# A fifth buffer for the probabilities of an attention stage, and one subtraction moved from VectorE to GpSimd

## The chip, the cores and the metric

The kernel runs on one core of a Trainium2 chip. The metric is the device time of one execution in microseconds, from a program that does everything in one launch. Engines are named as the profile names them: PE is TensorE's matmul, PEld its weight load, DVE is VectorE, ACT is ScalarE, POOL is GpSimd, SP is SyncE, whose queue issues most DMAs.

## The reference

Three parts in a row. Attention comes first, over 2 batches of 8 heads with 768 positions of 64 values: queries and keys are hashed to 6 bits by the signs of a projection, and a query sees only the keys of its own bucket.

```python
mask = q_bucket[:, :, :, None] == k_bucket[:, :, None, :]
scores = scale * np.matmul(q, k.transpose(0, 1, 3, 2))
scores = np.where(mask, scores, -1000000000.0)
scores = scores - np.max(scores, axis=-1, keepdims=True)
attn = np.exp(scores)
attn = attn / (np.sum(attn, axis=-1, keepdims=True) + 1e-09)
return np.matmul(attn, v).astype(np.float32)
```

Its rows go through a mixture of 8 experts (each token to one expert by a gate, two matmuls with a ReLU between), and the result through a dense layer of 2048 with `h * clip(h + 3, 0, 6) / 6`. All is fp32.

## The kernel before

fp32 accuracy is made from faster operand types: a number is split into a high half, rounded to the type of the operand, and a low half, the rest, and products of halves are summed. In attention a head's queries and keys come in as one tile `r` of 128 x 768 (64 rows of queries over 64 of keys). `halves` makes `hi` on ScalarE as `r` scaled by `SC`, and a tile for `lo`; the low half is `r * SC - hi`. It is made in `prep0` for heads 0 to 2 and in `prep` for the others. Four tiles of a set (X, Y, K1, K2; four sets, head modulo 4) get the halves: ScalarE writes the high ones of heads 0 to 2, `send_low` sends the low ones by two DMAs from SP's queue (L378, L379). `hi` (heads other than 1) and `lo` each have one buffer, so the next head's waits for the last one's readers.

For heads 0 and 1 GpSimd subtracts (L392) after ScalarE has made a scaled fp32 copy `x`. For head 2 VectorE does it in one instruction, scale and subtraction together (`low_half`, L374), as it does for all heads after it.

A head's 768 keys are 6 blocks, so there are 96 steps k over the 16 heads. In each step

- `mx` (eight steps ahead, more in the first steps) gives the row maxima: two matmuls (L456), each reduced by VectorE (L459), over three PSUM buffers. After a head's sixth block `turn` transposes the maxima and sends them from SP's queue as row 76 of that head's X (L470), where `scores` reads it;
- `scores` does four matmuls (L480, L481) into two PSUM buffers, and ScalarE takes the exponential of each half into `pf`, a block of fp32 probabilities of 128 x 768 (L482);
- `high` rounds `pf` to f16 on ScalarE (L487; every few blocks on VectorE, L489), and `low` subtracts on GpSimd (L493; at the end of the stage mostly on VectorE), which frees `pf`;
- `pv` multiplies the halves of two blocks with the values in every second step (L508 to L510).

The tag `pf` of pool `pt` has four buffers, taken in turn. Its first users, in program order, are `fill`, the scaled copy of head 0, `hi` of head 1, the scaled copy of head 1, and then the blocks 0, 1, 2 and so on.

The order of each engine's queue is written out by hand: straight code ahead of the loop (L744 to L812), then a loop over k in which `due(k)` runs what `at(...)` and `spread(...)` have put at a step or a fraction of one (table `Q`). Each engine works its queue in order. The scale of the values (`vscale`, a chain of small VectorE instructions and three small matmuls) ends with `isw` on VectorE (L649), and GpSimd copies that tile in place (L804) before it goes on to the loop. The low half of head 2 and its two sends stand at step 5.0, the load of the values of heads 4 to 7 (`load_v`, L599) at step 4.0.

After attention come the routing of the tokens, the experts (L1066 to L1302) and the dense layer (L1305 to L1455).

Of the kernel before, what the change touches and what calls it, by code (L numbers as in the profile page):

```python
# [9 lines left out]
F32 = mybir.dt.float32  # L10
F32R = mybir.dt.float32r
# [3 lines left out]
ALU = mybir.AluOpType  # L15
# [4 lines left out]
P = 128  # L20
B, H, S, D = 2, 8, 768, 64
NH = B * H
BITS = 6
NC = S // P
# [4 lines left out]
E = 8  # L29
# [13 lines left out]
SC = 2.0**-17  # L43
# [20 lines left out]
def moe_attention_kernel(ctx, tc, qk, v, vt, pj, wg, w1, w2, win, wout, out, cap):  # L64
    nc = tc.nc
    pe, act, dve, pool, sp = nc.tensor, nc.scalar, nc.vector, nc.gpsimd, nc.sync
# [3 lines left out]
    def opened(stack, name, bufs, side="left", **kw):  # L70
        return stack.enter_context(tc.tile_pool(name=name, bufs=bufs, side=side, reuse_waits="tile", **kw))

    def f32(t):
        return t.bitcast(F32)

    def run(gen):
        for _ in gen:
            pass
# [104 lines left out]
    def rtile(shape, name, dt=F32):  # L183
        return r1.tile([P] + shape, dt, tag=name, name=name)

    def bc(a, n):
        return a.unsqueeze(len(a.shape)).to_broadcast(list(a.shape) + [n])

    def mid(a, n):
        return a.unsqueeze(1).to_broadcast([a.shape[0], n] + list(a.shape[1:]))  # L190

    oh = rtile([B, NC, E], "oh", F16)
    rs = rtile([B, E], "rs", F16)
# [122 lines left out]
    with ExitStack() as actx:  # L316
# [3 lines left out]
        pt = opened(actx, "pt", 2)  # L320
# [33 lines left out]
        pf_t, phi_t, plo_t, pv_t, xp_t = {}, {}, {}, {}, {}  # L354
        vr_t, vt_t, vh_t, am_t, sc_t, sw_t = {}, {}, {}, {}, {}, {}

        def misc(name):
            return ps_x.tile([P, 512], F32, tag="x", name=name)

        def load_r(h):  # L360
            rt[h] = pr.tile([P, S], F32, tag="r", name=f"r{h}")
            sp.dma_start(out=rt[h], in_=qk[h])

        def halves(h):
            r = rt[h]
            if h == 1:
                hi = pt.tile([P, S], F32, tag="pf", name=f"hi{h}", bufs=4).bitcast(F32R)
            else:
                hi = ph.tile([P, S], F32R, tag="hi", name=f"hi{h}", bufs=1)
            act.activation(hi, r, AF.Copy, scale=SC)  # L370
            return r, hi, ph.tile([P, S], F32R, tag="lo", name=f"lo{h}")

        def low_half(lo, r, hi):
            dve.scalar_tensor_tensor(out=lo, in0=r, scalar=SC, in1=f32(hi), op0=ALU.mult, op1=ALU.subtract)  # L374

        def send_low(h, lo):
            st = sets[h % 4]
            sp.dma_start(out=f32(st["K1"])[D:P], in_=f32(lo)[D:P])  # L378
            sp.dma_start(out=f32(st["Y"])[0:D], in_=f32(lo)[0:D])  # L379

        def prep0(h):

            r, hi, lo = halves(h)
            if h < 2:
                x = pt.tile([P, S], F32, tag="pf", name=f"rs{h}", bufs=4)
                act.activation(x, r, AF.Copy, scale=SC)
            for n, d, o in (("X", 0, 0), ("K2", 0, D), ("K1", 0, D), ("Y", D, 0)):
                if h or n in ("K1", "Y"):
                    act.activation(sets[h][n][d : d + D], r[o : o + D], AF.Copy, scale=SC)
            yield  # L390
            if h < 2:
                pool.tensor_tensor(out=lo, in0=x, in1=f32(hi), op=ALU.subtract)  # L392
            else:
                low_half(lo, r, hi)
            yield
            send_low(h, lo)

# [74 lines left out]
        def scores(k):  # L472
            h, j = divmod(k, NC)
            st = sets[h % 4]
            pf = pf_t[k] = pt.tile([P, S], F32, tag="pf", name=f"pf{k}", bufs=4)
            kc = slice(j * P, (j + 1) * P)
            for n in range(2):
                ps = ps_t.tile([P, 512], F32, tag="t", name=f"pst{k}{n}")
                qc = slice(n * HS, (n + 1) * HS)
                pe.matmul(ps[:, :HS], st["K1"][:, kc], st["Y"][:, qc], start=True, stop=False)  # L480
                pe.matmul(ps[:, :HS], st["K2"][0:77, kc], st["X"][0:77, qc], start=False, stop=True)  # L481
                act.activation(pf[:, qc], ps[:, :HS], AF.Exp, scale=0.125 / SC / SC)  # L482
# [64 lines left out]
        def rows_of(r):  # L547
            b, k = divmod(r, KD)
            return xd[1 + b * S : 1 + (b + 1) * S, k * P : (k + 1) * P].rearrange("(p c) d -> p c d", c=NC)
# [113 lines left out]
        def unmatched(r):  # L663

            b, k = divmod(r, KD)
            rows = rows_of(r)
            n = 2 * NC * D
            vt = pr.tile([P, S], F32, tag="r", name=f"uv{r}").rearrange("p (h c d) -> p h c d", h=2, c=NC)
            sp.dma_start(out=vt.rearrange("p h c d -> p (h c d)"), in_=v[:, r * n : (r + 1) * n])
            last = r == NH // 2 - 1  # L670
            if not last:
                x = pr.tile([P, S], F32, tag="r", name=f"ux{r}").rearrange("p (c d) -> p c d", c=NC)
                sp.dma_start(out=x, in_=rows)
            m = pt.tile([P, S], F32, tag="pf", name=f"um{r}", bufs=4)
            ps = misc(f"psu{r}")
            for c in range(NC):
                pe.matmul(ps[:, 0:P], ones, vt[:, :, c], start=c == 0, stop=c == NC - 1)
            act.activation(m[:, 0:P], ps[:, 0:P], AF.Copy, scale=1.0 / S)
            ps = misc(f"psc{r}")
            pe.transpose(ps[:, 0:P], m[:, 0:P], ident)  # L680
            act.activation(m[:, P : 2 * P], ps[:, 0:P], AF.Copy, scale=SW)
            ps = misc(f"psl{r}")
            pe.matmul(
                ps[:, 0 : 2 * E], m[:, P : 2 * P], wg_sb[:, k, 0:2].rearrange("p h e -> p (h e)"), start=True, stop=True
            )
            z = nm[:, 2 * r : 2 * r + 2].rearrange("p h c -> p c h")
            y = pt.tile([P, S], F32, tag="pf", name=f"uy{r}", bufs=4).rearrange("p (c h d) -> p c h d", c=NC, h=2)
            dve.tensor_tensor(
                out=y, in0=bc(z, D), in1=mid(m[:, 0:P].rearrange("p (h d) -> p h d", h=2), NC), op=ALU.mult
            )  # L690
            if last:

                x = xp_t[r][:, :, E : E + D]
                dve.tensor_tensor(out=x, in0=x, in1=y[:, :, 0], op=ALU.add)
                sp.dma_start(out=rows[:, :, 0:D], in_=x)
                x = pv_t[2 * r + 1][:, 0 : NC * VA].rearrange("p (c d) -> p c d", d=VA)
                t, n = y[:, :, 1], nm[:, 2 * r + 1]
                dve.tensor_scalar(
                    out=t, in0=t, scalar1=sc_t[r // 2][:, 0:1], scalar2=float(S), op0=ALU.mult, op1=ALU.mult
                )  # L700
                dve.tensor_tensor(out=x[:, :, 0:D], in0=x[:, :, 0:D], in1=t, op=ALU.add)
                dve.scalar_tensor_tensor(
                    out=x[:, :, DE], in0=n, scalar=float(S), in1=x[:, :, DE], op0=ALU.mult, op1=ALU.add
                )
            else:
                dve.tensor_tensor(out=x, in0=x, in1=y.rearrange("p c h d -> p c (h d)"), op=ALU.add)
                sp.dma_start(out=rows, in_=x)
            y = pt.tile([P, S], F32, tag="pf", name=f"uz{r}", bufs=4)[:, 0 : NC * 2 * E]
            y = y.rearrange("p (c h e) -> p c h e", c=NC, h=2)
            dve.tensor_tensor(  # L710
                out=y, in0=bc(z, E), in1=mid(ps[:, 0 : 2 * E].rearrange("p (h e) -> p h e", h=2), NC), op=ALU.mult
            )
            for hh in range(2):
                dve.tensor_tensor(out=lg[:, b], in0=lg[:, b], in1=y[:, :, hh], op=ALU.add)
# [26 lines left out]
                pool.tensor_copy(c, c)  # L741


        fill = pt.tile([P, S], F32, tag="pf", name="fill", bufs=4)  # L744
        neg, zrow = fill[0:1], fill[32:33]
        pool.memset(neg, -1.0)
        pool.memset(zrow, 0.0)
# [14 lines left out]
        pre = [prep0(h) for h in range(3)]  # L762
        for n in range(2):
            for i, t in enumerate(("X", "K2")):
                c = slice(n * HS, (n + 1) * HS)
# [39 lines left out]
        heat(ps_v, "v", 2)  # L805
        mx(NC)
        run(pre[1])
        load_r(4)
        put_bits(2)
        first = vsplit(0), vgate(0)  # L810
# [22 lines left out]
        def at(k, f, *args):  # L833
            later.setdefault(k, []).append((f, args))
# [11 lines left out]
        def stages(gen, ks):  # L846
            for k in ks:
                at(k, next, gen, None)

        stages(first[0], (2, 2))  # L850
        stages(first[1], (2, 2.5, 3, 3.5, 4.5))
        at(5.0, run, pre[2])
        for i in range(3):
            at(Q["lr"][i], load_r, 5 + i)
        for g in range(1, G):
# [18 lines left out]
        for h in range(NH):  # L874
            k = NC * h + NC - 1 + LAG
# [63 lines left out]
        h = NH - 1  # L939
# [251 lines left out]
    def heat(n):  # L1191
# [23 lines left out]
        out=gates, in0=ps2[:, :, NW:], scalar=1.0 / LS, in1=gates, op0=ALU.mult, op1=ALU.add  # L1215
# [37 lines left out]
    for e in range(E):  # L1253
# [30 lines left out]
        for s in range(KF):  # L1284
            d, half = divmod(s, 2)
# [173 lines left out]
    with ExitStack() as octx:  # L1459
        op = opened(octx, "op", 1)  # L1460
# [128 lines left out]
```

## Time and profile before

| | us |
|---|---|
| median of 3 runs | 653.27 |
| lowest and highest | 651.11, 654.57 |
| the profiled execution | 653.98 |
| its span, first to last instruction | 652.3 |
| TensorE busy in the span | 623.4 |
| VectorE busy | 478.8 |
| ScalarE busy | 435.9 |
| GpSimd busy | 234.0 |

The durations that are used come from the profiled execution; what it took beyond its span lies around the first and last instruction. A matmul's duration holds its way through the array, so matmuls overlap, and a busy TensorE is read together with its waits. Attention takes the first third of the span.

### The profile page before, as it was taken

The numbers are of one execution on the slowest core, as the hardware profiler recorded it, in microseconds if no ns is written. First come the engines' busy times: TensorE is split into PE (matmuls) and PEld (weight loads), VectorE is DVE, ScalarE is ACT, GpSimd is POOL, SyncE is SP. The second block draws the span as 40 slices with busy tenths as digits, with TensorE's granted clock in tenths as the row PEclk, the third lists the DMA queues.
The fourth block names the chain that finished last, engine by engine and source line by source line (L and its number), as shares of the span: only waits on it lengthen the run. The fifth ranks groups of instructions, "written<-read, shape, count | busy, mean of one in ns | idle before, by whom it ended". The sixth has DMA issues, their size and how long they took to land.

```text
span 652.3 us, 14467 instructions
## 1 busy us (share of the span) xinstructions
PE 623.4 (96%) x5530; PEld 452.5 (69%) x5530; DVE 478.8 (73%) x1056; ACT 435.9 (67%) x882; POOL 234.0 (36%) x222
## 2 busy tenths in 40 slices
PE   8999999999998799999999999999999999999892
PEld 3678788788887589999999985555555555555441
DVE  6889998898999888888988887888887332222410
ACT  8878888788888657677777745554445685555820
POOL 6666978978994142210866100000000020000021
PEclk9999999999999999999999999999999999999997
DMA  6658568656474188877677553444440020000011
GB/s 196 204 137 230 166 159 230 167 132 179 100 203 145 36 286 276 250 248 238 207 241 252 164 170 117 135 129 140 151 131 31 1 81 17 1 1 0 2 50 53
DMA packets 35732, 92.19 MB, mean 141 GB/s; under 512 B 6778, under 2 KB 12250, under 8 KB 35650
## 3 DMA queue, kind: packets, MB, share of 16 engines
q1 hardware_dynamic: 32562, 83.75, 43.2%
q0 software_dynamic: 2400, 7.36, 3.4%
q8 instruction: 46, 0.75, 0.5%
q14 instruction: 36, 0.29, 0.1%
q10 hardware_dynamic: 688, 0.03, 0.1%
HBM read 67.14 MB, written 6.29 MB: 113 GB/s over the span
## 4 chain that ended last, share of the span: by engine, by line
PE 56%; DMA 4%; ACT 3%; issue 1%; DVE 1%; POOL 0%; POOLq 0%; DVEq 0%; ACTq 0%
PE psg L1363 17%; PE pso L1390 15%; PE psy L1141 11%; PE psh L1114 11%; DMA out_dram<-os,inv 3%; ACT junk L1317 2%; PE psa L1091 1%; ACT gh L1373 1%; DVE rl L1366 1%; DMA xg<-xd,ids 1%; DMA xd<-xp 1%; ACT rl L1365 0%; POOL xg L1072 0%; ACT xp L944 0%; POOL out_dram L1405 0%
## 5 line engine op out<-in xcount | busy, mean ns | idle before, releaser
L493 POOL TENSOR_TENSOR plo<-pf,phi 128x768 f16<-128x768 f32 x86 | 145.3, 1713 | 19.7 <-DVE phi L489 10.0
L1405 POOL DMA_INDIRECT out_dram<-os,inv x12 | 12.1, 1012 | 272.6 <-DVE os L1397 244.5
L482 ACT ACTIVATE pf<-pst 128x384 f32<-128x384 f32 x192 | 83.1, 486 | 30.0 <-PE pst L481 25.3
L459 DVE TENSOR_REDUCE mx<-psm 128x1 f32<-128x384 f32 x192 | 96.0, 546 | 6.8 <-PE psm L456 6.6
L164 DVE SCALAR_TENSOR_TENSOR wl<-raw,wh 128x1024 f16<-128x1024 f32 (+1 forms) x68 | 83.4, 1230 | 5.8 <-ACT wh L158 5.1
L1363 PE MATMUL psg<-yTh,ch 128*128 128x512 f16 (+1 forms) x256 | 83.4, 326 | 3.2 <-DVE rl L1366 3.2
L1363 PE MATMUL psg<-yTl,ch 128*128 128x512 f16 (+1 forms) x256 | 83.4, 326 | 0.0
L1363 PE MATMUL psg<-yTh,cl 128*128 128x512 f16 (+1 forms) x256 | 83.4, 326 | 0.0
L1366 DVE SCALAR_TENSOR_TENSOR rl<-rl,psg 128x512 f32<-128x512 f32 x64 | 35.0, 551 | 64.4 <-ACT rl L1365 64.0
L480 PE MATMUL pst<-Y,K 128*128 128x384 f32 x192 | 74.9, 390 | 2.5 <-ACT pf L482 2.5
L1363 PEld LDWEIGHTS <-ch 128*128 128x128 f16 x512 | 50.1, 98 | 35.9
L487 ACT ACTIVATE phi<-pf 128x768 f16<-128x768 f32 x85 | 71.7, 844 | 1.9
L1390 PE MATMUL pso<-ch,gh 128*128 128x512 f16 x192 | 72.8, 379 | 0.0
L1390 PE MATMUL pso<-ch,gl 128*128 128x512 f16 x192 | 72.8, 379 | 0.0
L1390 PE MATMUL pso<-cl,gh 128*128 128x512 f16 x192 | 72.8, 379 | 0.0
L158 ACT ACTIVATE wh<-raw 128x1024 f16<-128x1024 f32 (+1 forms) x68 | 67.4, 998 | 0.5 <-issue 0.5
L1390 PEld LDWEIGHTS <-gh 128*128 128x128 f16 x384 | 37.6, 98 | 42.3
L1141 PE MATMUL psy<-hh,wl 128*128 128x224 f16 x256 | 66.3, 259 | 0.0
L1141 PE MATMUL psy<-hl,wh 128*128 128x224 f16 x256 | 66.3, 259 | 0.0
L1141 PE MATMUL psy<-hh,wh 128*128 128x224 f16 x256 | 66.3, 259 | 0.0
L481 PE MATMUL pst<-X,K 77*128 77x384 f32 x192 | 65.4, 341 | 0.6 <-DMA X<-rm 0.6
L508 PE MATMUL psv<-vh,phi 128*128 128x73 f16 x576 | 64.0, 197 | 0.0
(251 smaller groups left out, 1477.2 us busy)
## 6 DMA issues: line engine op xcount, KB each, us to landing
raw<-in_w_dram SPq DMA_DIRECT2D x64, 512.0 KB
rc<-in_win_dram SPq DMA_DIRECT2D x16, 512.0 KB
rc<-in_wout_dram SPq DMA_DIRECT2D x16, 512.0 KB
r<-in_qk_dram SPq DMA_DIRECT2D x16, 384.0 KB
K<-hi SPq DMA_DIRECT2D x26, 192.0 KB
vr<-in_v_dram SPq DMA_DIRECT2D x4, 768.0 KB
vt<-in_vt_dram SPq DMA_DIRECT2D x8, 384.0 KB
K<-lo SPq DMA_DIRECT2D x16, 192.0 KB
```

Of the source, the lines that this page charges most:

```text
L158: act.activation(wh[e, i][:, c : c + n], r, AF.Copy, scale=(S1, S2)[i // 2])
L164: dve.scalar_tensor_tensor(out=wl[e, i][:, c : c + n], in0=r, scalar=(S1, S2)[i // 2], in1=wh[e, i][:, c : c + n], op0=ALU.mult, op1=ALU.s ...
L459: dve.tensor_reduce(out=mm[:, c, n : n + 1], in_=ps[:, :HS], axis=AX.X, op=ALU.max)
L480: pe.matmul(ps[:, :HS], st["K1"][:, kc], st["Y"][:, qc], start=True, stop=False)
L481: pe.matmul(ps[:, :HS], st["K2"][0:77, kc], st["X"][0:77, qc], start=False, stop=True)
L482: act.activation(pf[:, qc], ps[:, :HS], AF.Exp, scale=0.125 / SC / SC)
L487: act.activation(phi_t[k], pf_t[k], AF.Copy)
L493: eng.tensor_tensor(out=plo_t[k], in0=pf_t.pop(k), in1=phi_t[k], op=ALU.subtract)
L1114: pe.matmul(ps, l[:, c], r[:, k], start=n == 0, stop=n == 3 * KD - 1)
L1141: pe.matmul(ps, l, r, start=n == 0, stop=n == 3 * KF - 1)
L1363: pe.matmul(ps, l, x, start=n == 0, stop=n == 3 * KD - 1)
L1390: pe.matmul(po[blk][s], l, r, start=first and n == 0, stop=last and n == 2)
```

## The change

The tag `pf` gets a fifth buffer. The low half of head 2 is made as those of heads 0 and 1 are, in two instructions, but both on GpSimd: it scales `r` into a `pf` buffer (the fifth in turn) behind the low half of head 1, and subtracts behind the copy of `isw`. The sends of that low half go from step 5.0 to step 4.0, where they stand ahead of the load of the values of heads 4 to 7.

```diff
         def halves(h):
             r = rt[h]
             if h == 1:
-                hi = pt.tile([P, S], F32, tag="pf", name=f"hi{h}", bufs=4).bitcast(F32R)
+                hi = pt.tile([P, S], F32, tag="pf", name=f"hi{h}", bufs=5).bitcast(F32R)
...
             r, hi, lo = halves(h)
+            x = pt.tile([P, S], F32, tag="pf", name=f"rs{h}", bufs=5)
             if h < 2:
-                x = pt.tile([P, S], F32, tag="pf", name=f"rs{h}", bufs=4)
                 act.activation(x, r, AF.Copy, scale=SC)
+            else:
+                pool.tensor_scalar(out=x, in0=r, scalar1=SC, scalar2=None, op0=ALU.mult)
...
             yield
-            if h < 2:
-                pool.tensor_tensor(out=lo, in0=x, in1=f32(hi), op=ALU.subtract)
-            else:
-                low_half(lo, r, hi)
+            pool.tensor_tensor(out=lo, in0=x, in1=f32(hi), op=ALU.subtract)
             yield
             send_low(h, lo)
...
-            pf = pf_t[k] = pt.tile([P, S], F32, tag="pf", name=f"pf{k}", bufs=4)
+            pf = pf_t[k] = pt.tile([P, S], F32, tag="pf", name=f"pf{k}", bufs=5)
...
         run(pre[1])
+        next(pre[2])
         load_r(4)
...
-        at(5.0, run, pre[2])
+        at(4.0, run, pre[2])
```

The other lines of the diff give the same number of buffers where `pf` is taken elsewhere (`fill`, and `unmatched`, which these inputs don't run).

## Rows read from the trace of the kernel before

**Rows 1.** Stretch of attention: length, busy us (x instructions) by engine, granted clock, DMA share, GB/s.

```profile
42.00:200.00 158.00, 155.20 (x1961) 128.02 (x1962) 146.88 (x353) 134.18 (x250) 136.50 (x105) 1.00 0.65 173
```

**Rows 2.** Waits: who waited for whom, us in total, times, longest; 42 to 200, whole run.

```profile
PE psm L456 <- DVE mx L459: 1.0, 4, 0.5
DVE mx L459 <- PE psm L456: 5.9, 15, 0.8
...
ACT pf L482 <- POOL plo L493: 2.6, 3, 1.7
```

**Rows 3.** VectorE's timeline, 30 to 38 us: start, duration, what [idle before it, releaser].

```profile
30.21 3.41 DVE L374 SCALAR_TENSOR_TENSOR lo<-r,hi 128x768 fp32r<-128x768 f32 x1
...
37.43 0.96 DVE L374 SCALAR_TENSOR_TENSOR lo<-r,hi 128x768 fp32r<-128x768 f32 x1 [1.00 <-DMA Y<-lo]
```

**Rows 4.** GpSimd's timeline, 14 to 37 us.

```profile
14.01 1.81 POOL L392 TENSOR_TENSOR lo<-rs,hi 128x768 fp32r<-128x768 f32 x1 [0.58 <-DMA Y<-lo]
...
21.26 0.19 POOL L804 COPY isw<-isw 128x1 f32<-128x1 f32 x1 [5.43 <-DVE isw L649]
...
23.87 4.87 POOL L493 TENSOR_TENSOR plo<-pf,phi 128x768 f16<-128x768 f32 x3
...
29.55 3.25 POOL L493 TENSOR_TENSOR plo<-pf,phi 128x768 f16<-128x768 f32 x2
35.37 1.65 POOL L493 TENSOR_TENSOR plo<-pf,phi 128x768 f16<-128x768 f32 x1 [2.56 <-issue]
```

**Rows 5.** TensorE's timeline, 29 to 36 us.

```profile
29.25 0.21 PE L508 MATMUL psv<-vh,phi 128*128 128x73 f16 x1
...
31.31 0.39 PE L481 MATMUL pst<-X,K 77*128 77x384 f32 x1
...
33.19 0.33 PE L456 MATMUL psm<-K,X 76*128 76x384 f32 x1
34.16 1.36 PE L456 MATMUL psm<-K,X 76*128 76x384 f32 x3 [0.64 <-DVE mx L459]
35.37 0.21 PE L508 MATMUL psv<-vh,phi 128*128 128x73 f16 x1
```

**Rows 6.** ScalarE's timeline: the fifth block of probabilities.

```profile
25.81 0.87 ACT L482 ACTIVATE pf<-pst 128x384 f32<-128x384 f32 x2 [0.56 <-PE pst L481]
```

**Rows 7.** SP's queue: the load of values, and the row of maxima of heads 1, 4, 8.

```profile
23.18 0.42 SPq L599 DMA_DIRECT2D vr<-in_v_dram  x1
29.36 0.73 SPq L470 DMA_DIRECT2D X<-rm  x1
...
68.11 0.77 SPq L470 DMA_DIRECT2D X<-rm  x1
...
117.34 0.76 SPq L470 DMA_DIRECT2D X<-rm  x1
```

**Rows 8.** Stretches behind three rows of maxima and over head 2's sends; columns as rows 1.

```profile
29.40:32.40 3.00, 3.00 (x47) 2.37 (x44) 3.00 (x3) 1.39 (x3) 3.00 (x3) 1.00 0.04 17
68.10:71.10 3.00, 3.00 (x46) 2.59 (x46) 2.96 (x8) 2.62 (x5) 2.52 (x4) 1.00 0.63 228
117.30:120.30 3.00, 2.72 (x44) 2.23 (x43) 2.96 (x10) 2.65 (x5) 2.49 (x3) 1.00 0.55 198
34.50:36.50 2.00, 1.96 (x36) 1.51 (x36) 1.92 (x5) 1.49 (x4) 1.13 (x1) 1.00 0.78 202
```

**Rows 9.** Weight loads of TensorE that read the row of maxima, heads 4 and 8.

```profile
70.70 0.19 PEld L481 LDWEIGHTS pst<-X,K 77*128 77x128 f32 x1 [0.16 <-DMA X<-rm]
...
120.43 0.19 PEld L481 LDWEIGHTS pst<-X,K 77*128 77x128 f32 x1 [0.67 <-DMA X<-rm]
```

**Rows 10.** ScalarE's and TensorE's timelines near the end of attention.

```profile
207.99 0.87 ACT L482 ACTIVATE pf<-pst 128x384 f32<-128x384 f32 x2 [1.70 <-POOL plo L493]
...
209.64 0.85 ACT L482 ACTIVATE pf<-pst 128x384 f32<-128x384 f32 x2
...
209.07 0.34 PE L481 MATMUL pst<-X,K 77*128 77x384 f32 x1
```

More of the change, by code (lines that the diff above doesn't have):

```diff
@@ L673, in unmatched @@
                 sp.dma_start(out=x, in_=rows)
-            m = pt.tile([P, S], F32, tag="pf", name=f"um{r}", bufs=4)
+            m = pt.tile([P, S], F32, tag="pf", name=f"um{r}", bufs=5)
             ps = misc(f"psu{r}")
@@ L686, in unmatched @@
             z = nm[:, 2 * r : 2 * r + 2].rearrange("p h c -> p c h")
-            y = pt.tile([P, S], F32, tag="pf", name=f"uy{r}", bufs=4).rearrange("p (c h d) -> p c h d", c=NC, h=2)
+            y = pt.tile([P, S], F32, tag="pf", name=f"uy{r}", bufs=5).rearrange("p (c h d) -> p c h d", c=NC, h=2)
             dve.tensor_tensor(
@@ L707, in unmatched @@
                 sp.dma_start(out=rows, in_=x)
-            y = pt.tile([P, S], F32, tag="pf", name=f"uz{r}", bufs=4)[:, 0 : NC * 2 * E]
+            y = pt.tile([P, S], F32, tag="pf", name=f"uz{r}", bufs=5)[:, 0 : NC * 2 * E]
             y = y.rearrange("p (c h e) -> p c h e", c=NC, h=2)
@@ L741, in vsplit @@
                 pool.tensor_copy(c, c)
-        fill = pt.tile([P, S], F32, tag="pf", name="fill", bufs=4)
+        fill = pt.tile([P, S], F32, tag="pf", name="fill", bufs=5)
         neg, zrow = fill[0:1], fill[32:33]
```

## The prediction

> **What bounds the kernel now.** The change touches only the attention stage, which ends near 219 us of a 652.3 us span, so I read that stage and ask which engine paces it. In the table of stretches, between 42 and 200 us TensorE is busy 155.2 of 158 us, VectorE 146.9, GpSimd 136.5 and ScalarE 134.2 [rows 1]: four engines near full, so busy time alone doesn't decide. The waits of the same stretch do [rows 2]. VectorE's row maxima wait for TensorE 15 times (5.9 us); TensorE waits for them 4 times (1.0 us). ScalarE's waits for GpSimd to give back a buffer of probabilities come to 2.6 us in the whole run, three times. So TensorE's own queue paces the stage, and what VectorE, ScalarE or GpSimd save counts only where TensorE waits for it.
>
> One such place is early, in VectorE's timeline [rows 3]. The low half of head 2, a subtraction that takes 0.96 us for head 3, takes 3.41 us for head 2 (30.21 to 33.62). GpSimd's timeline says why [rows 4]: two of its subtractions for the probabilities stand back to back from 29.55 to 32.80, and VectorE's instruction ends 0.8 us after the second. It was held for 2.45 us. Behind it in VectorE's queue stand the row maxima of head 2, and TensorE needs their three PSUM buffers back: after its matmul at 33.19 it sits idle until 34.16, then runs three at VectorE's pace (1.36 us), and the products with the values, which follow in its queue, start at 35.37 [rows 5].
>
> **The change part by part.** (1) *The subtraction leaves VectorE.* Without the held instruction the first two reductions run while TensorE does the scores (before 33.2), the third starts when the matmul of 33.19 ends (33.52) and takes some 0.5 us (three take 1.36 with overlap). The sixth matmul needs only the buffer of the third reduction, free at about 34.1, and the products start near 34.25 instead of 35.37: **1.1 us**. It can't be more than 1.4: the matmul of 33.19 is followed by three more of the kind, and at the 0.2 us at which scores follow each other (31.31, then 33.19 with eight in between) they would end at 34.0. Nor is it nothing, since the TensorE wait is seen. The wait of 1.00 us ahead of head 3's subtraction, for the sends of head 2's low half [rows 3], goes too, but VectorE is then ahead of TensorE, so I count nothing; what may come back is that head 3's subtraction now starts beside GpSimd's work and is held for up to one instruction of 1.65 us, which ends about where the old one ended (38.39).
>
> Here a rule can be weighed. Row: VectorE's instruction came 0.66 us into GpSimd's first subtraction and got through only after the second [rows 3, 4]. The Trainium skill, "SBUF — State Buffer", section "Who interferes with whom", says that a VectorE instruction with two SBUF inputs and a GpSimd instruction that reads SBUF exclude each other, and that the second to issue blocks until the first finishes. By that alone head 2's subtraction would have ended 1.6 us earlier, at about 32.0, and TensorE would not have waited: the gain of (1) is then the row's bad luck, and head 3's subtraction can have it again. The sum goes by the row.
>
> (2) *GpSimd gets two instructions.* The scaling stands behind the low half of head 1, which ends at 15.82; from there GpSimd is idle 5.43 us until the scale of the values is ready at 21.26 [rows 4]. No row has this scaling; it costs between nothing (a scaling hidden in 5.43 us) and, at the 1.81 us of the two-input form of the same size, still nothing. Its target is the fifth buffer, never used before, so it waits for no one. The subtraction goes behind that scale: 1.81 us at 21.45, to 23.3. All that is queued behind it moves by as much: the first low probabilities, the low half of the values of head 0, the next probabilities. The second block, whose products come with the first, is done at 25.5 now [rows 4], 27.3 then; TensorE asks at 29.25 [rows 5]. GpSimd's later idle stretch of 2.56 us before 35.37 [rows 4] absorbs the delay. The scaled copy holds its buffer until 23.3, and the fifth block of probabilities, which takes that buffer, is written at 25.81 [rows 6]. Cover: 2 to 2.5 us on each; without it TensorE would stand for the excess. Cost taken: 0, at most 0.5 if the sends of head 1's low half land late.
>
> (3) *Two sends move.* The two transfers of head 2's low half (192 KB each) leave SP's queue behind 33.6 us and go ahead of the load of the values of heads 4 to 7, issued at 23.18 [rows 7]. SP reaches them just as the subtraction ends, so its queue loses at most their issue, about 1.2 us, and its next urgent issue is at 29.36. That one is the point: the row of maxima of head 1, which the scores need. TensorE reads it at 31.31 [rows 5], 1.95 us after issue. The load before it ends just then: the DMA engines' share from 29.4 to 32.4 is 0.04 [rows 8]. The two sends (with two small ones) take 0.78 of 2 us [rows 8], 1.6 us of all engines; put ahead, this work is left over behind 29.4. Two heads show what a full queue does to the same transfer: with 0.63 of 3 us to do it is read 2.59 us after issue (head 4, 68.11 to 70.70), with 0.55 of 3 us 3.09 us (head 8, 117.34 to 120.43, weights idle 0.67) [rows 7 to 9]. So between 0 (the queue drains in time) and 1.1 us later; with 1.7 us left over the case lies between those two, and I take **0.8 us**. TensorE stands at that matmul, so all of it is lost.
>
> (4) *Five buffers.* A block may be written once the one five back, not four back, is done. Of the three waits of 2.6 us in all, 1.70 is one wait at 207.99 [rows 10]. But the next scores are then not ready before 209.41 (matmul at 209.07, 0.34 us) and ScalarE takes them at 209.64; written earlier, they could go at about 209.45. **0.2 us** of it reaches the end. Bounds: 0 (VectorE's last subtractions bind) and 1.7. The other two waits share 0.9 us, and ScalarE's alone don't move TensorE: nothing.
>
> Sum: −1.1 + 0.8 − 0.2 = **−0.5 us**. Behind attention the chain is the same and follows it. The profiled execution took 653.98 us (span 652.3, the rest around it), 0.7 above the median of 653.27, which was one of runs from 651.11 to 654.57. Applied to the profiled time that is 653.5, to the median **652.8 us**.
>
> **The rivals.** *The row of maxima isn't delayed* (chance 0.20): what is left of the load runs beside it on few engines. For: head 4 lost only 0.16 us of idle [rows 9]. Then −1.1 − 0.2, with up to 0.7 more from the last buffer: 651.5.
>
> *VectorE was the bound* (0.12): then the whole 3.41 us and the 1.00 us wait count, −4.4, and the median is 648.9. For: 146.9 of 158 us busy. Against: it waits for TensorE six times as long as TensorE for it [rows 2].
>
> *The sends hold the row of maxima completely* (0.13), the side of slower. If the transfers drain strictly in turn, the row lands when all 1.7 us left over are done: 1.7 − 1.1 = 0.6 later at the products, 0.2 back at the end, +0.4, 653.7. It decides from a delay of 1.3 us on (1.1 + 0.2). Against: head 8, as much in the queue, 1.1 us. The Trainium skill, "DMA: Bandwidth & Descriptors", section "Two DMAs through the same engine are not ordered", has it that descriptors of one queue on one engine start in order, which speaks for this rival; the trace half agrees (0.67 us idle at head 8, 0.16 at head 4).
>
> *More than that slower* (0.05): the subtraction on GpSimd is held beyond 25.1 us by the sends of head 1, SP stands with it, and the fifth block and the first products wait in turn.
>
> **How the numbers follow.** The forecast above has the remaining 0.50; its own range, by the bounds (1.1 to 1.4; 0 to 1.1; 0 to 0.7), is 651.2 to 653.3 on the median. Half a per cent is 3.3 us, about what this kernel's runs can tell from no change: its three runs differ by 3.5. All cases but the second rival and the last lie within it, so same has 0.82. Faster has 0.13 (the second rival, and a little scatter), slower 0.05. The range reaches from between the first two rivals to the third plus the scatter of a median: 650.0 to 654.8.
>
> **What would show it.** After: no subtraction for head 2 on VectorE, and no TensorE wait between the row maxima near 33 us; GpSimd with a scaling near 16 us, a 1.8 us subtraction near 21.5 us and its idle stretch near 33 us shorter; the matmul at 31.3 us up to 1 us later, waiting for the row of maxima; products of the third and fourth block 0.3 us earlier than 35.37; no wait of ScalarE for GpSimd near 208 us. The forecast is wrong if the matmul at 31.3 isn't later (the first rival), if the lead at the products grows over the following heads (the second), or if TensorE stands at 29.25 for GpSimd.

## The result and the profile after

The changed kernel takes 657.43 us (median of 22 runs, 652.17 to 661.17), the kernel before 653.28 (22 runs, 651.11 to 656.27); the ratio is 1.0057, with a 95% interval of 1.004 to 1.0073. It is slower by about half a per cent where 652.8 was forecast. Two of the executions used below are far longer than all others, 2206.51 us (the seventh experiment, e7) and 896.46 us (the kernel before beside e5 to e8), and they stand in no median and no ratio. The profiled execution took 658.35 us with a span of 656.6, 4.3 more than before. Busy times of the page after (us, share, instructions) have TensorE 2.7 us up and VectorE 2.9 down, where the subtraction of 3.41 us left it:

```profile
PE 626.1 (95%) x5530; PEld 456.0 (69%) x5530; DVE 475.9 (72%) x1055; ACT 435.3 (66%) x882; POOL 237.5 (36%) x224
```

GpSimd's two new instructions are where they were expected. GpSimd's timeline after:

```profile
15.54 2.16 POOL L388 TENSOR_SCALAR rs<-r 128x768 f32<-128x768 f32 x1
20.59 0.19 POOL L803 COPY isw<-isw 128x1 f32<-128x1 f32 x1 [2.89 <-DVE isw L648]
20.77 1.83 POOL L393 TENSOR_TENSOR lo<-rs,hi 128x768 fp32r<-128x768 f32 x1
...
36.83 1.64 POOL L492 TENSOR_TENSOR plo<-pf,phi 128x768 f16<-128x768 f32 x1 [2.91 <-issue]
```

The scaling is hidden in GpSimd's wait for `isw`, which shrinks from 5.43 to 2.89 us, and a later idle stretch of 2.91 us is still there [rows 4]. Nobody waits for them.

SP's queue after (start, issue time, line), then TensorE's timeline:

```profile
22.63 0.54 SPq L378 DMA_DIRECT2D K<-lo  x1
23.22 1.57 SPq L379 DMA_DIRECT2D Y<-lo  x1
24.84 0.57 SPq L598 DMA_DIRECT2D vr<-in_v_dram  x1
28.67 0.76 SPq L469 DMA_DIRECT2D X<-rm  x1
```

```profile
30.25 0.53 PE L479 MATMUL pst<-Y,K 128*128 128x384 f32 x1
33.85 0.41 PE L480 MATMUL pst<-X,K 77*128 77x384 f32 x1 [3.07 <-DMA X<-rm]
34.10 0.34 PE L479 MATMUL pst<-Y,K 128*128 128x384 f32 x1
34.28 0.34 PE L480 MATMUL pst<-X,K 77*128 77x384 f32 x1
34.46 0.67 PE L455 MATMUL psm<-K,X 76*128 76x384 f32 x2
34.93 0.66 PE L479 MATMUL pst<-Y,K 128*128 128x384 f32 x1
35.39 0.52 PE L480 MATMUL pst<-X,K 77*128 77x384 f32 x1
```

Head 1's row of maxima is issued at 28.67 and read at 33.85, 5.2 us later; before it was read 1.95 us after issue and TensorE did not wait [rows 5, 7]. TensorE now stands 3.07 us for it. And the matmuls right behind take longer: the same `pst<-X,K` is 0.34 at 34.28 and 0.52 at 35.39. The table of stretches says why (length, busy us by engine, granted clock, DMA share, GB/s):

```profile
28.67:31.67 3.00, 2.11 (x41) 1.51 (x38) 0.96 (x3) 0.83 (x1) 3.00 (x3) 1.00 0.93 250
34.00:35.00 1.00, 1.00 (x6) 0.75 (x6) 0.15 (x1) 0.64 (x2) 0.00 (x0) 0.83 0.00 0
35.00:41.00 6.00, 5.99 (x47) 5.28 (x47) 3.69 (x7) 2.46 (x5) 1.64 (x1) 0.50 0.55 139
41.00:42.00 1.00, 1.00 (x5) 0.79 (x4) 0.03 (x1) 0.32 (x1) 0.00 (x0) 0.76 0.86 203
42.00:200.00 158.00, 155.90 (x2000) 128.44 (x1999) 147.41 (x355) 133.98 (x251) 135.49 (x103) 1.00 0.63 169
...
228.00:232.00 4.00, 1.80 (x15) 0.85 (x13) 3.30 (x14) 0.00 (x0) 3.23 (x3) 1.00 0.34 85
232.00:236.00 4.00, 3.91 (x16) 2.25 (x14) 2.28 (x6) 0.54 (x1) 1.69 (x3) 0.58 0.65 197
```

Three things are to be seen. In the 3 us behind the row's issue the DMA engines are 0.93 busy, where before they were all but empty (0.04, [rows 8]). Behind TensorE's idle time the granted clock is 0.50, the lower of its two levels (1.2 of 2.4 GHz), for the whole stretch from 35 to 41. It falls a second time behind a wait in the routing (0.58 from 232 to 236). From 42 to 200 the busy times are within 1.1 us of those of before [rows 1].

### The profile page after: what moved, and what is told of

Its sections match the earlier page's. It is cut to its first block, busy times and chain, and to the rows that moved or that the text cites. A ratio compares the mean times of both kernels' runs of the same rounds, so it can differ in the third digit from the quotient of the medians.

```text
span 656.6 us, 14466 instructions
## 1 busy us (share of the span) xinstructions
PE 626.1 (95%) x5530; PEld 456.0 (69%) x5530; DVE 475.9 (72%) x1055; ACT 435.3 (66%) x882; POOL 237.5 (36%) x224
## 4 chain that ended last, share of the span: by engine, by line
PE 55%; DVE 3%; ACT 3%; DMA 3%; issue 1%; POOL 0%; POOLq 0%; DVEq 0%
PE psg L1363 17%; PE pso L1390 15%; PE psy L1141 11%; PE psh L1114 10%; DMA out_dram<-os,inv 3%; ACT junk L1317 2%; PE psa L1091 1%; DVE wl L164 1%; ACT gh L1373 1%; DVE rl L1366 1%; PE heat L1193 0%; ACT rl L1365 0%; DVE hl L1118 0%; POOL out_dram L1405 0%; ACT wh L158 0%
```

## How the kernels are compared

VectorE's reduction `top<-mx` comes once for each head, when its row maxima are complete. The time from head 1's to head 2's holds the row's wait and the clock behind it, and nothing of what comes earlier. VectorE's timeline, the two `top` instructions of the kernel before, of the changed kernel, of a second profile of the kernel before (the eleventh experiment), and of the first and the fifth experiment:

```profile
28.49 0.17 DVE L462 TENSOR_REDUCE top<-mx 128x6 f32<-128x18 f32 x1
41.27 0.17 DVE L462 TENSOR_REDUCE top<-mx 128x6 f32<-128x18 f32 x1
```

```profile
27.80 0.17 DVE L461 TENSOR_REDUCE top<-mx 128x6 f32<-128x18 f32 x1
45.09 0.17 DVE L461 TENSOR_REDUCE top<-mx 128x6 f32<-128x18 f32 x1
```

```profile
28.69 0.17 DVE L462 TENSOR_REDUCE top<-mx 128x6 f32<-128x18 f32 x1
40.17 0.17 DVE L462 TENSOR_REDUCE top<-mx 128x6 f32<-128x18 f32 x1
```

```profile
28.46 0.17 DVE L461 TENSOR_REDUCE top<-mx 128x6 f32<-128x18 f32 x1
39.94 0.17 DVE L461 TENSOR_REDUCE top<-mx 128x6 f32<-128x18 f32 x1
```

```profile
27.97 0.17 DVE L461 TENSOR_REDUCE top<-mx 128x6 f32<-128x18 f32 x1
42.38 0.17 DVE L461 TENSOR_REDUCE top<-mx 128x6 f32<-128x18 f32 x1
```

The table has this interval (A) for every kernel, worked out in this way, beside TensorE's wait for the row, the granted clock from 35 to 41, and two more intervals: B from head 2's `top` to head 15's (the rest of attention), C from there to the first activation of the experts (`hh<-psh`, ScalarE), which holds the routing. Medians and ratios are over all runs but those two, the ratio against runs of the kernel before on the same chip. A, B and C are from one profiled execution each.

| kernel | A | wait | clock | B | C | median | ratio, 95% |
|---|---|---|---|---|---|---|---|
| before, first profile | 12.78 | 0 | 1.00 | 159.62 | 33.28 | 653.28 | |
| before again (e11) | 11.48 | 0 | 1.00 | 159.60 | 32.84 | 652.63 | 0.9999, 0.9979 to 1.002 |
| changed kernel | 17.29 | 3.07 | 0.50 | 158.96 | 34.21 | 657.43 | 1.0057, 1.004 to 1.0073 |
| e1 sends behind the row | 11.48 | 0 | 1.00 | 158.94 | 34.10 | 652.55 | 1.0004, 0.999 to 1.0017 |
| e2 fifth buffer alone | 11.48 | 0 | 1.00 | 159.36 | 34.06 | 651.81 | 0.9996, 0.9979 to 1.0014 |
| e3 two more sends, before | 16.55 | 2.42 | 0.51 | 159.41 | 33.85 | 656.42 | 1.0055, 1.0031 to 1.008 |
| e4 load behind the row | 12.49 | 0.84 | 1.00 | 158.98 | 34.06 | 652.43 | 1.0002, 0.9987 to 1.0016 |
| e5 kept busy | 14.41 | 0 | 1.00 | 159.12 | 34.07 | 654.2 | 1.003, 1.0016 to 1.0044 |
| e6 load ahead of the sends | 13.77 | 2.11 | 1.00 | 159.00 | 32.83 | 655.25 | 1.0032, 1.0005 to 1.0059 |
| e7 row on another queue | 18.67 | 3.20 | 0.50 | 158.96 | 32.81 | 658.2 | 1.0077, 1.0058 to 1.0095 |
| e8 one send ahead | 13.51 | 1.85 | 1.00 | 158.96 | 33.17 | 653.63 | 1.0028, 1.0009 to 1.0047 |
| e9 before, routing busy | 11.48 | 0 | 1.00 | 159.46 | 32.75 | 651.59 | 0.999, 0.997 to 1.0011 |
| e10 e1, routing busy | 11.48 | 0 | 1.00 | 159.07 | 33.35 | 651.49 | 0.9974, 0.996 to 0.9988 |

## The experiments

The theory after the traces: the two sends in the queue ahead of the load and the row make the row late, TensorE stands, and its clock falls behind that. The rivals: GpSimd's extra work makes something late (A); the fifth buffer costs it (B).

**e1, the sends back behind the row.** The rest of the change stays.

```diff
-        at(4.0, run, pre[2])
+        at(5.0, run, pre[2])
```

> The changed kernel with one step put back: the two sends of head 2's low half are issued where they were before the change, behind the load of values and behind head 1's row of maxima; GpSimd's scaling and subtraction and the fifth buffer stay. Theory (the two sends ahead of the load make the row of maxima late, and TensorE's idle time and lower clock follow from that): the row lands near 31 us as before the change, TensorE waits for it 0 to 1 us instead of 3.07, its granted clock stays 1.00 from 34 to 42 us, and the time is 651 to 653 us. Rival A (GpSimd's extra work makes something late): 656 to 658 us, as the changed kernel. Rival B (the fifth buffer costs it): 656 to 658 us too.

652.55 us against 652.01 for the kernel before on the same chip: the whole loss is gone with this one step (ratio 1.0004, interval 0.999 to 1.0017). SP's queue and TensorE's timeline:

```profile
23.14 0.44 SPq L598 DMA_DIRECT2D vr<-in_v_dram  x1
29.32 0.73 SPq L469 DMA_DIRECT2D X<-rm  x1
30.15 0.55 SPq L378 DMA_DIRECT2D K<-lo  x1
```

```profile
30.91 0.53 PE L479 MATMUL pst<-Y,K 128*128 128x384 f32 x1
31.28 0.39 PE L480 MATMUL pst<-X,K 77*128 77x384 f32 x1
```

The row is read 1.96 us after issue, as before. Both rivals fall: GpSimd's work and the fifth buffer are in this kernel. The second half of it is as plain: with the subtraction off VectorE no gain over the kernel before can be measured.

A further rival was not tried by itself. With head 2's sends moved, the two small transfers of head 2's bits that stand behind them (36 KB each, `X<-b` and `K<-b`) also go out earlier, at 29.48 and 30.32 right behind the row, and could slow it. In e3, below, they go out at 33.31 and 34.17, when the row's last packet is through (33.17 by the packet records), and the row is late all the same; so they are not needed for the loss.

**e2, the fifth buffer alone**, in the kernel before (every `bufs=4` of the tag `pf` made 5).

> The kernel before with the fifth buffer of probabilities and nothing else of the change. Theory (late row of maxima): 652.8 to 653.5 us, the 1.70 us that ScalarE waited at 207.99 gone or halved and nothing else moved. Rival A (GpSimd's work): the same. Rival B (the fifth buffer costs it): 656 to 658 us.

651.81 against 652.01: no loss, and no gain that can be measured.

**e3, the suspected cost added to the kernel before.** The sends carry the high half at first, and it is overwritten.

```diff
             yield
+            if h == 2:
+                send_low(h, hi)
+                yield
...
+        at(4.0, next, pre[2])
         at(5.0, run, pre[2])
```

> The kernel before, with the low half of head 2 still subtracted by VectorE and sent where it was, but with two more sends of the same size put into the queue ahead of the load of values; they carry the high half into the places that the low half overwrites later, so that the result is the same. Theory (late row of maxima): the row lands 2 to 3 us later than before, TensorE waits for it 2 to 4 us, its granted clock falls behind that, and the time is 655.5 to 658.5 us although nothing on GpSimd and no buffer changed. Rivals A and B: 652.8 to 653.8 us.

656.42, ratio 1.0055, nearly that of the changed kernel, with no GpSimd instruction and no buffer changed. TensorE's timeline:

```profile
33.96 0.61 PE L484 MATMUL pst<-X,K 77*128 77x384 f32 x1 [2.42 <-DMA X<-rm]
```

**e4, the load of values behind the row**, the sends still ahead of it (`'lv': 5.0` in the table `Q`, from 4.0).

> The changed kernel with the load of values (six loads' place in the queue unchanged but this one) moved behind head 1's row of maxima; the two sends stay ahead of the row. It divides the theory: if the load, held up by the sends, is what the row waits behind, the row lands near 31 us, TensorE's clock stays 1.00 and the time is 651 to 653.5 us, unless the values are now late for their transposes (then 654 to 656). If the sends by themselves hold the row, it lands after 32.5 us, and the time is 655 to 657 us. Rivals A and B: 656 to 658 us.

TensorE waits 0.84 us, its clock stays, and the time is that of the kernel before (ratio 1.0002). So neither alone brings the whole wait: with the load but no sends ahead of the row there is none (e1), with the sends but no load 0.84, with both 2.11 to 3.07. The values were not missed where they now land.

**e5, the clock by itself.** 13 more filler matmuls stand in front of the scores that read the row.

```diff
             if k == NC:
-                heat(ps_v, "v", 3)
+                heat(ps_v, "v", 16)
```

> The changed kernel with 13 more filler matmuls (of the kind at 30.49 in the kernel before, 0.21 us apart, 2.8 us in all) in front of the scores that read head 1's row of maxima, so that TensorE works while it would wait. It prices the clock. Theory (the idle time itself costs some 2.5 us, and the lower clock behind it some 1.7 more): the granted clock stays 1.00 from 30 to 42 us, the stretch behind the row is no later than 3 us against the kernel before instead of 4.2, and the time is 655 to 656.3 us. Rival (the lower clock costs nothing, since something else sets the pace there): the time stays 656.8 to 658 us.

The row is read at 33.70, nearly as late as in the changed kernel, but the clock holds. TensorE's timeline and a stretch of e5:

```profile
33.70 0.41 PE L480 MATMUL pst<-X,K 77*128 77x384 f32 x1
```

```profile
35.00:41.00 6.00, 5.70 (x63) 4.33 (x63) 5.56 (x11) 4.13 (x9) 1.65 (x1) 1.00 0.62 156
```

TensorE runs 63 matmuls in those 6 us, 47 in the changed kernel. Interval A is 14.41 instead of 17.29. Split at the read of the row, it gives each its share. From the read to head 2's `top` it is 8.66 us in e1 and 8.68 in e5, with the late row and the clock at 1.00, but 11.24 in the changed kernel (33.85 to 45.09): the lower clock costs 2.6 us. From head 1's `top` to the read it is 2.82 us in e1, 5.73 in e5 and 6.05 in the changed kernel: the late row costs 3.2 us there. Together they are the 5.81 us over the 11.48 without a wait. The medians differ by 3.2 us (654.2 and 657.43), but each was measured beside other runs of the kernel before; by the two ratios it is 0.27%, 1.8 us. All 12 runs of e5 have a mean granted clock of 0.991 or more over the run. Of the 22 of the changed kernel only four have, and they took 652.17 to 654.86; the other 18, at 0.984 to 0.990, took 655.48 to 661.17. So the wide scatter of the changed kernel goes with the clock.

**e6, the load ahead of the sends** (`'lv': 3.9`): all three are still ahead of the row, in another order.

> The changed kernel with the load of values in front of the two sends instead of behind them; the row of maxima is behind all three as before. Theory A (all that stands in the queue ahead of the row counts, in any order): the row lands after 32.5 us and the time is 655 to 658 us. Theory B (the sends make the load behind them slow, so the order between them counts): the row lands before 32 us and the time is 651.5 to 654 us.

The row is read at 33.55, 4.2 us after issue, with 2.11 us of waiting: theory A of that expectation, what stands ahead counts in either order. The clock stayed in the profiled execution, which took 652.13; four of the twelve, with a mean granted clock of 0.984 to 0.990, took 655.6 to 661.09. The median of 655.25 lies at the lower end of what was expected, and the interval of its ratio is wide.

**e7, the row from another queue.**

```diff
-            sp.dma_start(out=row, in_=f32(rowm[h % 2]))
+            (act if h == 1 else sp).dma_start(out=row, in_=f32(rowm[h % 2]))
```

> The changed kernel with head 1's row of maxima issued by ScalarE, so on a queue without the load and the sends; nothing else moves. Theory A (the row waits for its turn behind the packets of its own queue): it lands within 2.5 us of its issue, TensorE waits less than 1 us for it, the clock stays 1.00, and the time is 651 to 653 us. Theory B (the 16 DMA engines are full, whichever queue it comes from): it still lands 4 to 5 us after its issue, and the time is 655 to 658 us.

658.2, no better. ScalarE's queue, TensorE's timeline and SP's queue:

```profile
29.55 1.30 ACTq L469 DMA_DIRECT2D X<-rm  x1
```

```profile
31.12 0.53 PE L479 MATMUL pst<-Y,K 128*128 128x384 f32 x1
34.84 0.66 PE L480 MATMUL pst<-X,K 77*128 77x384 f32 x1 [3.20 <-DMA X<-rm]
```

```profile
25.72 0.80 SPq L414 DMA_DIRECT2D X<-b  x1
26.60 0.76 SPq L415 DMA_DIRECT2D K<-b  x1
```

Read 5.3 us after issue, on a queue with nothing else in it (the issue itself comes 0.9 us later and is 0.5 longer than SP's). It is not all that moved, as the expectation had it: SP no longer waits to issue the row, so head 2's bits go out at 25.72 and 26.60, ahead of the row and not behind it (29.48 and 30.32 in the changed kernel), 72 KB more of work ahead of it. The packet records of the three traces, for the row's six packets of 512 bytes and the load's last packet:

```
                 row's packets start at (us)              load's last packet ends
before           30.73 30.73 30.74 30.75 30.76 30.79      30.06
changed kernel   31.20 31.47 31.52 31.97 32.20 33.04      33.04
e7               32.13 32.16 32.72 33.04 33.21 33.94      33.73
```

Before, the six start together; after, they go off one by one, about as the load drains, and the row is complete with the slowest, on its own queue too. So a queue of its own did not help the row while the DMA engines had this work in hand; what it would do without the bits ahead wasn't tried. The Trainium skill, "DMA: Bandwidth & Descriptors", section "Issuing engines are not separate DMA queues", says just this: a transfer that another engine issues runs on the same 16 DMA engines. The trace agrees (5.3 us from issue to use on ScalarE's queue, 5.2 on SP's).

**e8, one of the two sends ahead**, the other behind the row.

```diff
-            send_low(h, lo)
+            if h == 2:
+                st = sets[h]
+                sp.dma_start(out=f32(st["K1"])[D:P], in_=f32(lo)[D:P])
+                yield
+                sp.dma_start(out=f32(st["Y"])[0:D], in_=f32(lo)[0:D])
+            else:
+                send_low(h, lo)
...
-        at(4.0, run, pre[2])
+        at(4.0, next, pre[2])
+        at(5.0, run, pre[2])
```

> The changed kernel with only one of the two sends (the low half into the keys) ahead of the load of values and the row; the other (into the queries) goes behind the row. If the delay grows with the bytes ahead of the row, the row lands about half as late (1 to 2 us of waiting by TensorE), and the time is 652.5 to 655 us; if one send is as bad as two, the row lands near 33.8 us and the time is 656 to 658 us; if there is a slack that one send fits into, 651 to 653 us with no wait over 0.5 us.

TensorE waits 1.85 us, ratio 1.0028: half of the bytes cost more than half of the wait, and half of the time. The profile is the fastest of the twelve runs (651.76), with the clock at 1.00; four others, at 0.988 to 0.990, took 654.68 to 659.5.

**e9 and e10, the routing.** The second fall of the clock is not only the changed kernel's: in C, the kernels whose profile shows it there (changed kernel, e1 to e5) have 33.85 to 34.21, the others 32.75 to 33.35. Both kernels get nine fillers where TensorE waits for VectorE's gates (third entry of `'ht'` in `Q`, 7 to 16): e9 the kernel before, e10 the kernel of e1.

> The kernel before with 9 more filler matmuls (0.215 us apart, 1.94 us in all) in the routing, where TensorE waits 2.0 us for VectorE's gates ahead of the second window sum. In the changed kernel's profile the granted clock fell a second time behind that wait (0.58 from 232 to 236), in the profile of the kernel before it did not, and in those of three experiments that run as fast as before it did. Theory (that fall is a cost that both kernels pay in part of their executions and no effect of the change): the clock stays 1.00 there, and the median falls by 0.5 to 2 us against the kernel before. Rival (the fall costs nothing, since the experts' weights set the pace there): no difference over 0.3 us.

> The first experiment (changed kernel, the two sends back behind the load and the row of maxima) with the same 9 filler matmuls in the routing. If the routing's fall costs both kernels, it is 0.5 to 2 us faster than the kernel before, as the ninth, and the two lie within 0.7 us of each other. If GpSimd's subtraction is worth the 1.1 us of the prediction, this one is the faster of the two by about that.

The stretches of e1, then of e10:

```profile
224.00:228.00 4.00, 1.87 (x12) 0.69 (x12) 2.88 (x11) 0.00 (x0) 3.09 (x4) 0.90 0.50 145
228.00:232.00 4.00, 3.80 (x18) 2.58 (x18) 1.96 (x5) 1.51 (x3) 1.69 (x4) 0.67 0.72 202
```

```profile
224.00:228.00 4.00, 3.67 (x22) 1.48 (x20) 2.56 (x13) 0.00 (x0) 3.09 (x4) 1.00 0.43 123
228.00:232.00 4.00, 3.29 (x23) 2.29 (x24) 2.66 (x7) 2.03 (x3) 1.86 (x3) 1.00 0.68 172
```

The clock holds, in most runs too: all 12 of e10 and 11 of the 12 of e9 have a mean granted clock of 0.993 or more, against 12 of the 29 runs of the kernel before beside them. e10 is the one kernel here that is faster than the kernel before (0.9974, interval 0.996 to 0.9988, 651.49 us). e9's ratio of 0.999 can't be told from 1, though its median of 651.59 is within 0.1 us of e10's. Whether the subtraction on GpSimd brings the 1.1 us can't be read from this pair: by the medians the two are alike, by the ratios they are 0.16% (1.0 us) apart, with intervals that overlap. Interval A speaks against it, 11.48 in both.

**e11, the kernel before again**, for a second profile.

> The kernel before, unchanged, for a second profile. The prediction took VectorE's low half of head 2 at 3.41 us, from one execution. If that hold is the usual case, it is over 3 us here too; if it depends on where GpSimd's instructions happen to stand, it is near 1.8 us, as in the second experiment, and TensorE's score of head 2 follows 0.3 us after the one before it instead of 0.64.

VectorE's timeline:

```profile
30.40 1.80 DVE L374 SCALAR_TENSOR_TENSOR lo<-r,hi 128x768 fp32r<-128x768 f32 x1
```

1.80 us, not 3.41 [rows 3], and interval A is 11.48, as in e1, e2, e9 and e10 to the hundredth. The 3.41 belonged to one execution.

## Why the prediction was wrong

**Step 3, the two sends, failed by its size.** The mechanism was the one named, the row of maxima held by what the DMA engines have left; the term was 0.8 us, at most 1.1. TensorE read the row at 33.85 where it was ready for it at about 30.6 (0.36 us behind the matmul of 30.25, as 31.31 follows the one of 30.95 before): 3.2 us. The two heads that the bound was taken from (68.11 and 117.34, [rows 7, 8]) had 0.63 and 0.55 of 3 us of DMA work behind their issue, this one had 0.93. And the 1.7 us left over were reckoned as if the sends ran as fast as alone. They don't. Stretches of the changed kernel, then of the kernel before (columns as above): 23.5 to 25.0, where the sends run beside the loads, and the whole way from 5.0 us ahead of head 1's `top` to the end of the load:

```profile
23.50:25.00 1.50, 1.20 (x8) 0.96 (x7) 1.50 (x4) 1.03 (x2) 1.50 (x2) 1.00 0.87 125
22.80:33.10 10.30, 7.16 (x65) 5.09 (x64) 6.12 (x17) 6.05 (x12) 10.30 (x8) 1.00 0.87 235
```

```profile
23.50:25.00 1.50, 1.20 (x7) 0.84 (x7) 0.90 (x2) 1.47 (x4) 1.50 (x2) 1.00 0.86 328
23.50:30.10 6.60, 5.78 (x50) 4.30 (x50) 5.89 (x16) 5.95 (x12) 6.60 (x6) 1.00 0.81 303
```

The engines were as busy and moved less, 125 GB/s instead of 328 at the worst, 235 instead of 303 over the whole way. That way takes 10.3 us instead of 6.6. By these rates 2.42 MB went instead of 2.00: an estimate from them gives 1.4 of the 3.7 us to the added bytes (0.42 MB at 303 GB/s) and 2.3 to the lower rate. The rate goes with the sends: over the same way it is 247 GB/s in e3 and 260 in e6, but 298 in e1 and e11, which have no sends there. Why the engines move less while they are as busy stays open. The third rival (the sends hold the row completely) was nearest, and its 1.7 us were half of what came.

**A term was missing: the clock.** No step asked what TensorE does after it has stood. e5 prices it at 2.6 us of interval A, beside 3.2 for the late row. The Trainium skill, "TensorE: Matmul & The Clock Gate", section "HAM oscillation — how this bites in real kernels", tells of a loop whose waits for transfers bring the lower clock to the work behind each. Here the trace agrees (0.50 from 35 to 41, behind 3.07 us of idling), and e5 shows the other side (1.00 with the same late row).

**Step 1, the subtraction off VectorE (−1.1), was right for that execution and not for the kernel.** With the sends out of the way (e1) the change does make A shorter than in the profile that the prediction read, by 1.30 us (12.78 to 11.48). But the kernel before has 11.48 too when VectorE's instruction isn't held over two of GpSimd's, as in e2, e9 and e11 (1.80 to 1.82 us; e3, the fifth profile with it on VectorE, has 1.81). The prediction said so itself, as a possibility ("the row's bad luck"), and summed by the row. In the changed kernel, head 3's subtraction wasn't held (0.95 us at 38.78); in e1 it was (1.63 us), with no loss.

**Step 2, GpSimd at no cost, was right**, by its own rows and by e1.

**Step 4, the fifth buffer (−0.2), brought nothing where it was looked for.** The wait of 1.70 us at 207.99 [rows 10] is gone in e2, and the last exponential starts 0.1 us earlier behind head 15's `top` (13.54 us instead of 13.66). But the last product of attention does not. TensorE's timeline, kernel before and e2:

```profile
218.45 0.20 PE L510 MATMUL psv<-vh,plo 128*128 128x73 f16 x1
```

```profile
216.18 0.20 PE L510 MATMUL psv<-vh,plo 128*128 128x73 f16 x1
```

They stand 17.56 and 17.57 us behind head 15's `top` (200.89 and 198.61): the prediction's lower bound of 0. e2's ratio of 0.9996 has an interval of two tenths of a per cent to either side. In the changed kernel and e1 ScalarE's waits for GpSimd's `low` to give back a buffer, 2.6 us before [rows 2], are gone; in e2 1.7 us of them are left, at other places, so the fifth buffer alone does not end them. Interval B is 159.41 to 159.62 with four buffers, 159.36 with five alone, and 158.94 to 159.12 with the whole change in any order of the sends: some 0.5 us that the prediction didn't have. What of the change brings it wasn't tried and stays open.

**The account.** Against the second profile of the kernel before, up to the first activation of the experts: −0.89 in the front (27.80 and 28.69 for head 1's `top`; e2 and e9, whose front is unchanged, have 27.77 and 27.79, so this is scatter), +5.81 in A, −0.64 in B, +1.37 in C, together +5.65 us, 238.26 against 232.61. The spans differ by 6.7 us (656.6 and 649.9); the 1.05 us behind that point were not followed. This is one execution against one: by the medians the change costs 4.15 us. The profile that the prediction read lies later by its hold in A (1.30) and in C (0.44). C is the clock in the routing, which either kernel pays in some executions.

## What to carry to other kernels

Before a transfer is moved ahead of another in time, ask which small transfer, read by the pacing engine, is issued while the moved bytes are still under way: here it was as late as the last of its six packets, from either of two queues. A wait of TensorE has to be priced with the clock behind it, which here cost 2.6 us on top of 3.2. Fillers in the wait gave back only the clock's part (e5, ratio 1.003); the sends (e1) or the load (e4) put behind the small transfer gave back the whole. A single long instruction in one profile is no price until a second profile shows it.

## What had not been expected of the hardware

- Two sends within SBUF (192 KB each, 3 KB packets) beside loads brought the DMA engines from 328 to 125 GB/s at a share of 0.87 busy over 1.5 us, and from 303 to 235 GB/s until the load was through.
- A 3 KB transfer became late by the load on the DMA engines on a queue of its own too (5.3 us from issue to use, 5.2 on the shared one; with 72 KB more ahead of it).
- In the profiled executions the granted clock fell behind TensorE waits for the row of 2.42, 3.07 and 3.20 us and stayed behind those of 0.84, 1.85 and 2.11. In the routing, waits of 2.0 to 2.2 us did either: it stayed at 1.00 in the first profile of the kernel before and fell in that of e3, both behind 2.0 us.
- GpSimd's scaling of 128 x 768 fp32, with one input, took 2.16 us, longer than the subtraction with two (1.83).
- VectorE's fp32 subtraction of one size took 0.95, 1.30 (e4), 1.63 (e1), 1.80 (e11) and 3.41 us. The 3.41 stood beside two of GpSimd's instructions back to back [rows 3, 4]; what stood beside the others was not compared.
